# A first item of the expert phase with a table of its own, and five more split tiles: one core of Trainium2

## The chip, the cores and the metric

The kernel runs on one core of a Trainium2 chip. The core has five engines that run their own instruction streams in order and wait for each other by semaphores: TensorE (PE in the profile; its weight loads are PEld), VectorE (DVE), ScalarE (ACT), GpSimd (POOL) and SyncE (SP), of which SP and POOL issue the transfers here. The metric is the time of one execution on the device, in microseconds (us).

## What is computed

Four batches of attention across channels (B = 4, N = 3648 rows, C = 256 channels), and on its 14592 output rows a mixture of 16 experts, each row going to one of them:

```python
qn = q / (norm(q, axis=1) + 1e-06); kn = k / (norm(k, axis=1) + 1e-06)
s = kn.transpose(0, 2, 1) @ qn / tau            # 256 x 256 for each batch
a = softmax(s); x = (v @ a).reshape(B * N, C)
g = argmax(x @ w_group); e = argmax(x @ w_expert[g])    # one of 4 x 4 experts for each row
out[row] = p_group * p_expert * (relu(x[row] @ w1[g, e]) @ w2[g, e])
```

## The kernel before

**Units.** A batch is cut into 28 tiles of 128 rows and one of 64, four tiles to a unit; a batch has eight units (GPB = 8), of which the last holds the 64 rows. Units are counted through, 0 to 31; batch 2 is units 16 to 23, batch 3 units 24 to 31.

**Phase 1, on unit u.** s_load (L184) loads q and k of the unit into `qkraw`. s_split (L198, L199) takes some of its tiles apart into a high and a low half: ACT writes the high half and DVE subtracts. Tile 3 (SPLIT) goes to `qkhi`/`qklo`; the tiles listed in MORE go to `hh`/`hl`, of which there are three buffers. ACT squares the unit, and s_add (L216) adds the squares up in `sqa`. s_mm (L232) multiplies into `sacc`: a raw tile by two fp32 matmuls, which are four records in the trace, a split one by three matmuls of halves for each of two column blocks. At the end of a batch softmax has several steps: `ssq` on DVE (L243, L244) sums the squares, `nps` on PE (L247, L249) adds them over the partitions, `rn` takes the root and the reciprocal, `sm` scales `sacc`, and behind that come the exponentials and the weights `ahi`, `alo`.

**Phase 2, on unit x, ten units later.** x_load (L306) loads v, x_tr (L318 to L320) transposes it on PE into `vtr` and splits it into `vth` and `vtl`, and x_mm (L342) multiplies with `ahi` and `alo`; ACT copies the result to `xs` (L345). The routing (L369 to L439, DVE mostly) finds each row's expert and its place in the buffer x_sorted; it runs over ranges of tiles, in batch 2 over (0, 8), (8, 20) and (20, 29). `carry` counts the rows of each expert. The scatters (L466, POOL) write one tile of rows each into x_sorted.

**Phase 3.** The first items of 512 rows of one expert are chosen before all rows are routed. When the ranges up to (2, 20) are through (PRE), tables_pre makes the table tb_pre of four items (KPRE = 4): each full 512 rows of an expert give one. fetch_w (L677, L684) loads an item's weights and fetch_x (L697, L698) its rows of x_sorted; SP reads expert and place from the table first. The reads of these items wait for the scatters of the ranges below PRE, one for each tile: 29 of each of batches 0 and 1 and 20 of batch 2, which is 78. Later scatters are declared harmless to them. split_x (L779 to L781) transposes item 0's rows into `xtr` and splits them, split_w (L741, L742) splits its weights, and ffn1 (L930, `hmm`) and ffn2 (L950 to L959) follow.

**What sets the order.** The streams of SP and POOL are written out by hand throughout. PE, ACT and DVE are ordered by the scheduler up to step 30 (TM), which covers units 0 to 29 of phase 1, the sums and `ssq` of the last batch, and units 0 to 19 of phase 2; `sqa` and `ssq` of the last unit stand there under a raised priority (tc.high_priority, offset 400). Then all five engines run in the order of the code, and PE's first instructions there are `nps` of the last batch, the transposes of v and the matmuls of units 30 and 31.

Of the kernel before, what the change touches and what calls it, by code (L numbers as in the profile page):

```python
# [46 lines left out]

PRE = (2, 20)
assert 2 * NT + PRE[1] * P > E * (BIG - 1) + (KPRE - 1) * BIG
# [3 lines left out]
PLAIN = (GPB + 1, GPB + 2)  # L53
MORE = {**{u: (2,) for u in range(GPB + 6, 28)}, 28: (1, 2), 29: (0, 1, 2), 30: (0, 1, 2)}
US = UX = B * GPB
# [6 lines left out]
def attention_moe(ctx: ExitStack, tc, q, k, v, tau, w_group, w_expert, w1, w2, out):  # L62
# [288 lines left out]

    scatters, pend, now, rows_at, early, spread = [], [], [0], {}, [], []

# [94 lines left out]

    before = lambda r: r < PRE
    late = []  # L450

    def scatter(n, wait=0):
        for _ in range(n):
            if not pend or pend[0][1] + wait > now[0]:
                break
            (b, j0), _, j, si = pend.pop(0)
            g, t = divmod(j0 + j, GJ)
            rows, nj = rows_of(g)
            xs = rows_at[b, g]
            if t == 0:  # L460
                tok = xs[:, 0:nj, C].bitcast(I32)
                if g < NG:
                    POOL.iota(tok, pattern=[[-1, GJ]], base=NOID - b * NT - g * GJ, channel_multiplier=-J)
                else:
                    POOL.iota(tok, pattern=[[0, 1]], base=NOID - b * NT - J * P, channel_multiplier=-1)
            ins = POOL.indirect_dma_start(  # L466
                out=xs_d, out_offset=bass.IndirectOffsetOnAxis(ap=si[:rows, j:j + 1], axis=0),
                in_=xs[:rows, t, 0:RW].bitcast(I32), in_offset=None, bounds_check=NSLOT - 1, oob_is_err=False)
            if not before((b, j0)):
                for o in early:  # L470
                    tc.declare_no_dep(ins.ins, o, reason="the first items' slots have been filled")
                late.append(ins.ins)
            for o in scatters:
                tc.declare_no_dep(ins.ins, o, reason="every token has a slot of its own")
            scatters.append(ins.ins)
            pause()
# [80 lines left out]
    used = r16("used")  # L557

    def tables_pre():
        cnt = carry  # L560
        f = shifted(cnt, 9, "f1", "key")
        inc = r16("inc1", "order")
        DVE.tensor_tensor_scan(inc, onesf[:, 0:E], f, 0.0, ALU.mult, ALU.add)
        DVE.tensor_tensor(inc, inc, f, ALU.subtract)
        yield
        DVE.tensor_scalar(inc, inc, -1.0, float(KPRE), ALU.mult, ALU.add)
        DVE.tensor_scalar(inc, inc, 0.0, None, ALU.max)
        DVE.tensor_tensor(used, inc, f, ALU.min)
        full = r16("held1", "full")
        DVE.tensor_scalar(full, used, float(BIG), None, ALU.mult)  # L570
        yield
        return (yield from table_steps(KPRE, used, ecap, full, BIG, "pre"))

    def zero_rows():
# [3 lines left out]
        DVE.tensor_tensor(end, end, own, ALU.mult)  # L578
        ends = rp.tile([P, 1], F32, name="ends")
        DVE.tensor_reduce(ends, end, AX.X, ALU.add)  # L580
# [4 lines left out]
                                in_=zero[:3 * E, :].bitcast(I32), in_offset=None, bounds_check=NSLOT - 1, oob_is_err=False)  # L585
        for o in scatters + early:
            tc.declare_no_dep(ins.ins, o, reason="these slots have no token")
        scatters.append(ins.ins)
        late.append(ins.ins)

# [95 lines left out]
    def fetch_x(d, tb, i):  # L686
# [5 lines left out]
        d["nv"] = tb[1][:, i:i + 1]  # L692
        if tb is not tb_pre:
            gather(d["xg"].rearrange("p t w -> p (t w)"), tb[2][:, i:i + 1], 4)
            pause()
            return
        s = SP.value_load(tb[0][0:1, i, 1:2], min_val=0, max_val=DUMMY)  # L697
        ins = SP.dma_start(d["xg"].bitcast(I32), xs_d[ds(s, BIG), :].rearrange("(p t) w -> p t w", t=4))  # L698
        early.append(ins.ins)
        for o in late:  # L700
            tc.declare_no_dep(ins.ins, o, reason="the first items' slots have been filled")

# [100 lines left out]
    xs_at = {t: t - XOFF if t >= XOFF else None for t in range(UX + XOFF)}  # L803
    tb_pre = tb_big = tb_pc = tb_sub = nsub = None

# [5 lines left out]
    def queue(x):  # L811
        b, g = divmod(x, GPB)
        for j0, j1 in RANGES[b]:
            if (b, j1) != (B - 1, NJ) and j1 == min(NJ, (g + 1) * GJ) and (g < NG - 1 or j1 == NJ):
                if not (j1 == NJ and g == NG - 1):
                    rgens.append(routing(b, j0, j1))
                    if (b, j1) == PRE:
                        rgens.append(pre_gen())
# [49 lines left out]
    def where(i):  # L868
        return (items[i], tb_pre, i) if i < KPRE else (items[i], tb_big, i - KPRE)

# [14 lines left out]
    for t in range(TM, len(xs_at)):  # L885
# [18 lines left out]
        if k == 8:  # L904
            fetch_w(items[0], tb_pre, 0, "w1")
            fetch_x(items[0], tb_pre, 0)
            fetch_w(items[0], tb_pre, 0, "w2")
        if k == 10:
            vx_.close()
            wb = ctx.enter_context(tc.tile_pool(name="wb", bufs=4))  # L910
        if x == UX - 1:
            fetch_x(items[1], tb_pre, 1)
            fetch_w(items[1], tb_pre, 1, "w1")
            split_x(items[0])
# [465 lines left out]
```

## Time and profile before

| | |
|---|---|
| time, median of three runs | 929.68 us (926.58, 929.68, 929.70) |
| the profiled execution | 926.72 us, span 924.9 us |
| granted clock of TensorE, mean | 0.996 |
| PE, PEld, DVE, ACT, POOL busy | 99%, 84%, 77%, 53%, 44% of the span |

The profile is of one execution. A row of waits gives the time that an engine stood idle before a line and what released it; a row of the timeline gives start, duration, engine, line, output and input, and in brackets the idle time ahead of it. The ends of matmuls are modelled, so their starts are the better measure. PEclk is the granted clock of TensorE as a share of full speed.

### The profile page before, as it was taken

How to read it: one execution, taken by the hardware profiler on the slowest of the kernel's cores; microseconds unless marked ns; L12 is line 12 of the kernel's file. 1: busy time of each engine (PE TensorE's matmuls, PEld its weight loads, DVE VectorE, ACT ScalarE, POOL GpSimd, SP SyncE). 2: the span in 40 equal slices, each digit the busy share in tenths (PEclk: the TensorE clock that was granted, in tenths of full speed). 3: DMA queues.
4: the chain of work that ended last, by engine and by line, in shares of the span. 5: the costliest groups of instructions: out<-in, count | busy, mean ns of one | idle time of the engine just before them, and what ended most of it. 6: DMA issues, size and time to landing. Idle time of an engine off the chain costs nothing.

```text
span 924.9 us, 17250 instructions
## 1 busy us (share of the span) xinstructions
PE 911.8 (99%) x5660; PEld 773.7 (84%) x5660; DVE 715.0 (77%) x1496; ACT 494.7 (53%) x831; POOL 403.8 (44%) x569
## 2 busy tenths in 40 slices
PE   8999999999999999999999999999999999999997
PEld 7899999999899988888888888888888888888885
DVE  6888999888799877967885777678776877587752
ACT  6788888777454444444444444444544444444432
POOL 0001898888588663323222333343334333332222
PEclk9999999999999999999999999999999999999998
DMA  9975779274855676767777777777777677667750
GB/s 310 353 285 193 264 263 319 95 248 144 294 195 175 193 250 225 232 228 235 248 249 239 257 251 246 249 245 232 227 223 244 224 250 233 220 236 241 244 165 32
DMA packets 159172, 213.97 MB, mean 231 GB/s; under 512 B 63107, under 2 KB 117643, under 8 KB 159072
## 3 DMA queue, kind: packets, MB, share of 16 engines
q1 hardware_dynamic: 144128, 168.23, 56.0%
q0 software_dynamic: 14944, 44.54, 12.8%
q8 instruction: 46, 0.75, 0.3%
q14 instruction: 54, 0.44, 0.2%
HBM read 170.33 MB, written 31.39 MB: 218 GB/s over the span
## 4 chain that ended last, share of the span: by engine, by line
PE 90%; DVE 3%; ACT 3%; DMA 2%; issue 1%; SPq 0%; POOL 0%; DVEq 0%; ACTq 0%
PE hmm L930 34%; PE wacc L950 19%; PE wacc L951 10%; PE xmm L342 7%; PE sacc L232 6%; PE yacc L959 5%; PE qacc L1067 2%; PE qmm L1054 2%; PE vtr L318 2%; DMA qkraw<-in_k 2%; DVE sqa L216 1%; ACT xs L345 1%; ACT sq L207 1%; PE xtr L779 1%; DVE vtl L320 1%
## 5 line engine op out<-in xcount | busy, mean ns | idle before, releaser
L939 ACT ACTIVATE hh<-hmm 128x512 fp32r<-128x512 f32 x222 | 133.4, 601 | 351.7 <-PE hmm L930 347.3
L930 PE MATMUL hmm<-xth,ww 128*128 128x512 f32 x896 | 317.6, 395 | 0.0
L979 POOL DMA_INDIRECT out<-ys,ids x112 | 132.9, 1187 | 386.7 <-DVE ys L968 357.6
L950 PE MATMUL wacc<-ww,hh 128*128 128x512 f32 x752 | 274.6, 399 | 0.0
L940 DVE SCALAR_TENSOR_TENSOR hl<-hmm,hh 128x512 fp32r<-128x512 f32 x222 | 152.7, 690 | 128.4 <-ACT hh L939 125.7
L951 PE MATMUL wacc<-ww,hl 128*128 128x256 f32 x752 | 210.8, 280 | 0.0
L930 PEld LDWEIGHTS hmm<-xth,ww 128*128 128x128 f32 x896 | 168.8, 188 | 38.1
L930 PE MATMUL hmm<-xtl,ww 128*128 128x512 f32 x448 | 177.7, 397 | 0.0
L950 PEld LDWEIGHTS wacc<-ww,hh 128*128 128x128 f32 x752 | 141.3, 188 | 43.0 <-DVE ys L968 8.2
L466 POOL DMA_INDIRECT x_sorted<-xs,si x112 | 137.2, 1225 | 56.9 <-DVE si L439 25.5
L742 DVE TENSOR_TENSOR ww<-wraw,ww 128x1024 fp32r<-128x1024 f32 x112 | 136.7, 1221 | 16.6 <-ACT ww L741 15.4
L951 PEld LDWEIGHTS wacc<-ww,hl 128*128 128x128 f32 x752 | 142.1, 189 | 7.2
L741 ACT ACTIVATE ww<-wraw 128x1024 fp32r<-128x1024 f32 x112 | 118.8, 1060 | 6.2 <-DMA wraw<-in_moe_w 6.1
L930 PEld LDWEIGHTS hmm<-xtl,ww 128*128 128x128 f32 x448 | 84.5, 189 | 9.7
L159 POOL MEMSET zero<- 128x256 f32 x260 | 87.1, 335 | 0.1
L232 PE MATMUL sacc<-qkraw 128*128 128x256 f32 (+1 forms) x280 | 69.5, 387 | 1.1 <-DMA qkraw<-in_k 1.1
L342 PE MATMUL xmm<-ahi,vth 128*128 128x276 f32 (+1 forms) x232 | 69.5, 304 | 0.3 <-ACT xs L345 0.3
L342 PE MATMUL xmm<-alo,vth 128*128 128x276 f32 (+1 forms) x232 | 67.8, 293 | 0.0
L342 PE MATMUL xmm<-ahi,vtl 128*128 128x276 f32 (+1 forms) x232 | 67.5, 292 | 0.0
L216 DVE TENSOR_TENSOR sqa<-sqa,sq 128x1024 f32<-128x1024 f32 (+3 forms) x46 | 59.9, 1309 | 6.1 <-ACT sq L207 3.8
L1039 DVE STREAM_TRANSPOSE qhT<-qh 32x128 f32<-32x128 f32 x192 | 57.7, 300 | 2.7
L232 PEld LDWEIGHTS sacc<-qkraw 128*128 128x128 f32 (+1 forms) x280 | 50.5, 192 | 7.8 <-issue 2.2
(276 smaller groups left out, 1357.2 us busy)
## 6 DMA issues: line engine op xcount, KB each, us to landing
wraw<-in_moe_w SPq DMA_DIRECT2D x55, 1024.0 KB
wraw<-in_moe_w SPq DMA_DIRECT2D x50, 512.0 KB
qw<-in_moe_w SPq DMA_DIRECT2D x48, 512.0 KB
vr<-in_v SPq DMA_DIRECT2D x28, 512.0 KB
qkraw<-in_q SPq DMA_DIRECT2D x26, 512.0 KB
qkraw<-in_k SPq DMA_DIRECT2D x26, 512.0 KB
xq<-xg SPq DMA_DIRECT2D x368, 32.0 KB
x_sorted<-xs,si POOLq DMA_INDIRECT x112, 3.9
```

The source lines that it names most:

```text
L159: POOL.memset(zero[:, 0:256], 0.0)
L232: PE.matmul(d["acc"][:, c, :], kt[:rows, 1, cs], qt[:rows, 0, :], start=d.pop("first", True) and c == 0, stop=(g == NG), skip_group_check= ...
L342: PE.matmul(mm[:rows, :NE], vt[:, c, j * P:j * P + rows], at[:, c, :], start=(n == 0), stop=(n == 5))
L466: ins = POOL.indirect_dma_start(out=xs_d, out_offset=bass.IndirectOffsetOnAxis(ap=si[:rows, j:j + 1], axis=0), in_=xs[:rows, t, 0:RW].bitc ...
L741: ACT.activation(h, r, AF.Copy)
L742: DVE.tensor_tensor(l, r, h, ALU.subtract)
L930: PE.matmul(mm, wt[:, c, fs], xt[:, c, :], start=(n == 0), stop=(n == 5))
L939: ACT.activation(hh, mm, AF.Relu)
L940: d["hl"] = DVE.scalar_tensor_tensor(hl, mm, 0.0, hh, ALU.max, ALU.subtract)
L950: PE.matmul(d["acc"][t].rearrange("p c n -> p (c n)"), hh[:, tsl], d["w2w"][:, f, :], start=(f == 0), stop=(f == 7), skip_group_check=True)
L951: PE.matmul(d["acc"][t][:, 0, :], hl[:, tsl], d["w2h"][:, f, :], start=False, stop=(f == 7), skip_group_check=True)
L979: ins = POOL.indirect_dma_start(out=out, out_offset=bass.IndirectOffsetOnAxis(ap=d["ids"][:, t:t + 1], axis=0), in_=d["ys"][:, t, :], in_o ...
```

## The change

Two edits. First, the table of item 0 is made earlier. After the routing of (2, 8), when the rows of 58 + 8 = 66 tiles are counted, table_first finds the first expert that has 512 rows (`ge0`, a running count, `one` marks that expert) and writes tb_first. Item 0 is read by that table, and its read waits for the scatters of the ranges below PRE0 = (2, 8) alone. tables_pre makes three items, from what is left when the rows of item 0 are taken off. Second, MORE has tile 1 as well in units 24 to 27 and tile 0 as well in unit 28, so that five tiles more run over halves.

```diff
-PRE = (2, 20)
+PRE0, PRE = (2, 8), (2, 20)
+assert 2 * NT + PRE0[1] * P > E * (BIG - 1)
-MORE = {**{u: (2,) for u in range(GPB + 6, 28)}, 28: (1, 2), 29: (0, 1, 2), 30: (0, 1, 2)}
+MORE = {**{u: (2,) for u in range(GPB + 6, 24)}, **{u: (1, 2) for u in range(24, 28)}, 28: (0, 1, 2), 29: (0, 1, 2), 30: (0, 1, 2)}
...
-            if not before((b, j0)):
-                for o in early:
+            for o, limit in early:
+                if (b, j0) >= limit:
                     tc.declare_no_dep(ins.ins, o, reason="the first items' slots have been filled")
-                late.append(ins.ins)
+            late.append((ins.ins, (b, j0)))
...
+    def table_first():
+
+        ge = r16("ge0", "order")
+        DVE.tensor_scalar(ge, carry, float(BIG), None, ALU.is_ge)
+        inc = r16("inc0", "key")
+        DVE.tensor_tensor_scan(inc, onesf[:, 0:E], ge, 0.0, ALU.mult, ALU.add)
+        DVE.scalar_tensor_tensor(one, inc, 1.0, ge, ALU.is_equal, ALU.mult)
+        DVE.tensor_tensor(ge, one, iof[:, 0:E], ALU.mult)
+        e0 = rp.tile([P, 1], F32, tag="ends", name="e0")
+        DVE.tensor_reduce(e0, ge, AX.X, ALU.add)
+        tb = rp.tile([P, 1, 2], I32, name="tb_first")
+        DVE.tensor_copy(tb[:, :, 0], e0)
+        DVE.tensor_scalar(tb[:, :, 1], e0, float(CAP), None, ALU.mult)
+        yield
+        return tb, full0
...
     def tables_pre():
-        cnt = carry
-        f = shifted(cnt, 9, "f1", "key")
+        f = r16("f1", "held2")
+        DVE.tensor_tensor(f, shifted(carry, 9, "key"), one, ALU.subtract)
...
-        return (yield from table_steps(KPRE, used, ecap, full, BIG, "pre"))
+        first = r16("first", "s0")
+        DVE.scalar_tensor_tensor(first, one, float(BIG), ecap, ALU.mult, ALU.add)
+        yield
+        tb = yield from table_steps(KPRE - 1, used, first, full, BIG, "pre")
+        DVE.tensor_tensor(used, used, one, ALU.add)
+        return tb
...
-        early.append(ins.ins)
-        for o in late:
-            tc.declare_no_dep(ins.ins, o, reason="the first items' slots have been filled")
+        limit = PRE0 if d is items[0] else PRE
+        early.append((ins.ins, limit))
+        for o, r in late:
+            if r >= limit:
+                tc.declare_no_dep(ins.ins, o, reason="the first items' slots have been filled")
...
                     rgens.append(routing(b, j0, j1))
+                    if (b, j1) == PRE0:
+                        rgens.append(first_gen())
...
     def where(i):
-        return (items[i], tb_pre, i) if i < KPRE else (items[i], tb_big, i - KPRE)
+        if i == 0:
+            return items[i], tb_first, 0
+        return (items[i], tb_pre, i - 1) if i < KPRE else (items[i], tb_big, i - KPRE)
```

The order of the instructions moves with it. The lines of the changed kernel are one higher than before up to the scatters.

On DVE, before, near the end of the part that the scheduler orders: the sums of squares of the last batch (L243, L244, `ssq`) stand among the routing of (2, 8), and the routing, the splits of v (`vtl`) and of q and k follow.

```order
L243 TENSOR_TENSOR sqa<-sqa 128x2x512
L378 SCALAR_TENSOR_TENSOR oh_2381<-z,key_99 128x160
L400 TENSOR_REDUCE sw<-ez 128x40
L379 TENSOR_REDUCE m_2377<-oh_2381 128x40
L244 TENSOR_TENSOR ssq<-sqa 128x512
L380 TENSOR_TENSOR oh_2381<-oh_2381,m_2377 128x160
L320 TENSOR_TENSOR vtl<-vtr,vth 128x512
```

The last rows of that part on DVE, before: splits of q and k and the end of the routing (`si`), and then the first row in hand order (`rn`).

```order
L199 TENSOR_TENSOR hl<-qkraw,hh 128x512
L434 TENSOR_TENSOR inc<-inc,oh 128x128
L199 TENSOR_TENSOR hl<-qkraw,hh 128x512
L437 TENSOR_REDUCE sf<-inc 128x8
L199 TENSOR_TENSOR hl<-qkraw,hh 128x512
L439 CAST si<-sf 128x8
L255 TENSOR_SCALAR rn<-rn 128x258
```

The same place on DVE now: the last sums and `ssq` (L217, L244, L245) stand behind the splits, the routing and the new table.

```order
L200 TENSOR_TENSOR hl<-qkraw,hh 128x512
L571 TENSOR_REDUCE e_2582<-ge_2576 128x1
L200 TENSOR_TENSOR hl<-qkraw,hh 128x512
L573 CAST tb_first<-e_2582 128x1
L574 TENSOR_SCALAR tb_first<-e_2582 128x1
L217 TENSOR_TENSOR sqa<-sqa,sq 128x1024
L217 TENSOR_TENSOR sqa<-sqa,sq 64x256
L244 TENSOR_TENSOR sqa<-sqa 128x2x512
L245 TENSOR_TENSOR ssq<-sqa 128x512
L256 TENSOR_SCALAR rn<-rn 128x258
```

What moved: `ssq` went from 24 rows ahead of the end of that part to its last row.

On PE, now, with its waits: the last matmuls of unit 19, then `nps`, which reads `ssq`, the transposes of v and the matmuls of unit 30.

```order
L343 MATMUL xmm<-ahi,vtl 128x276
L248 MATMUL nps<-ssq,onesf 128x256 [waits DVE_49]
L250 MATMUL nps<-onesf,ssq 128x1 x2
L319 MATMUL vtr<-ident,vr 128x128 [waits DMAHW0_49,PE_49]
L319 MATMUL vtr<-ident,vr 128x128 x3
L319 MATMUL vtr<-ident,vr 128x128 [waits PE_49]
L319 MATMUL vtr<-ident,vr 128x128 x3
L233 MATMUL sacc<-hh 128x256
```

What moved: nothing in the rows; the DVE row that `nps` waits for is the one that moved above.

On SP, before: the second half of item 0's weights and, behind it, the read of item 1's rows from x_sorted.

```order
L682 DMA wraw<-in_moe_w 128x4x256
L682 ISA
L682 DMA wraw<-in_moe_w 128x4x256 [waits DMAHW6_49]
L697 TENSOR_LOAD tb_pre
L697 ISA x2
L698 ISA
L698 DMA xg<-x_sorted 128x1088 [waits DMAHW7_49,DVE_49,Pool_49]
```

The same place on SP now.

```order
L705 DMA wraw<-in_moe_w 128x4x256
L705 ISA
L705 DMA wraw<-in_moe_w 128x4x256 [waits DMAHW6_49]
L720 TENSOR_LOAD tb_pre [waits DVE_49]
L720 ISA x2
L721 ISA
L721 DMA xg<-x_sorted 128x1088 [waits DMASW4_49,DMASW3_49,DMASW5_49,DMASW2_49,DMASW6_49,DMASW1_49,DMASW7_49,DMASW0_49,DMAHW7_49,DVE_49,Pool_49]
```

What moved: the waits for POOL's transfers (DMASW) of the range (8, 20) and for tb_pre stand at item 1 now; item 0's read keeps waits of that kind, for earlier transfers.

## Rows read from the trace of the kernel before

**Rows 1.** The page, busy time of each engine: us, share of the span, instructions.

```profile
PE 911.8 (99%) x5660; PEld 773.7 (84%) x5660; DVE 715.0 (77%) x1496; ACT 494.7 (53%) x831; POOL 403.8 (44%) x569
```

**Rows 2.** Waits of PE, 140 to 340 us: total, times, longest.

```profile
PE xtr L779 <- DMA wraw<-x_sorted: 3.1, 1, 3.1
PE vtr L318 <- DVE vtl L320: 0.3, 1, 0.3
PE atp L281 <- DVE ax L275: 0.2, 1, 0.2
```

**Rows 3.** Chain of work that ended last, 200 to 240 us: start, duration, what.

```profile
226.37 2.44 DMA x_sorted<-xs,si
...
229.08 4.03 DMA wraw<-x_sorted
...
233.25 1.39 PE xtr L779 x8
```

**Rows 4.** Windows: length; PE, PEld, DVE, ACT, POOL busy; PEclk; DMA share; GB/s.

```profile
233.20:234.00 0.80, 0.75 (x6) 0.78 (x7) 0.00 (x0) 0.00 (x0) 0.80 (x1) 1.00 0.96 302
234.00:235.00 1.00, 1.00 (x7) 0.99 (x7) 0.37 (x1) 0.92 (x2) 0.83 (x3) 0.54 0.96 290
235.00:236.00 1.00, 1.00 (x6) 0.98 (x5) 1.00 (x4) 0.28 (x1) 0.93 (x3) 0.50 1.02 230
236.00:237.00 1.00, 1.00 (x4) 0.81 (x3) 0.93 (x5) 0.61 (x2) 0.79 (x1) 0.50 0.92 333
237.00:238.00 1.00, 1.00 (x5) 0.72 (x5) 0.49 (x1) 0.00 (x0) 0.83 (x3) 0.75 1.05 406
```

**Rows 5.** Timeline of POOL: the scatter of the 66th tile.

```profile
207.91 0.97 POOL L466 DMA_INDIRECT x_sorted<-xs,si  x1 [0.16 <-DVE f L554]
```

**Rows 6.** Timeline of SP's queue: the last loads of v; item 1's read.

```profile
188.21 19.82 SPq L306 DMA_DIRECT2D vr<-in_v  x8
...
232.18 0.35 SPq L698 DMA_DIRECT2D xg<-x_sorted  x1
```

**Rows 7.** Timeline of DVE, 226 to 239 us: item 0's weights and tokens are split.

```profile
229.27 2.46 DVE L742 TENSOR_TENSOR ww<-wraw,ww 128x1024 fp32r<-128x1024 f32 x2 [0.58 <-ACT ww L741]
234.63 1.37 DVE L781 TENSOR_TENSOR xtl<-xtr,xth 128x512 fp32r<-128x512 f32 x2 [2.90 <-ACT xth L780]
```

**Rows 8.** Timeline of PE: two raw tiles of q and k, then matmuls of halves.

```profile
147.79 1.89 PE L232 MATMUL sacc<-qkraw 128*128 128x256 f32 x8
...
149.63 0.28 PE L232 MATMUL sacc<-hl,hh 128*128 128x256 f32 x1
149.75 0.28 PE L232 MATMUL sacc<-hh,hl 128*128 128x256 f32 x1
```

**Rows 9.** Windows ahead of nps, columns as in rows 4.

```profile
160.00:170.00 10.00, 10.00 (x80) 9.85 (x80) 9.93 (x30) 6.85 (x16) 9.06 (x12) 1.00 0.46 174
170.00:180.00 10.00, 9.91 (x82) 9.54 (x81) 9.82 (x30) 7.25 (x17) 9.07 (x12) 1.00 0.24 86
180.00:182.00 2.00, 2.00 (x17) 2.00 (x17) 1.90 (x6) 0.98 (x3) 1.83 (x3) 1.00 0.20 72
```

**Rows 10.** Timeline of DVE, 140 to 205 us.

```profile
173.96 0.67 DVE L244 TENSOR_TENSOR ssq<-sqa 128x512 f32<-128x512 f32 x1
...
178.91 0.15 DVE L431 TENSOR_TENSOR carry<-pp,carry 128x16 f32<-128x16 f32 x1
178.99 0.15 DVE L432 SCALAR_TENSOR_TENSOR bs<-bs,ecap 128x16 f32<-128x16 f32 x1
...
181.14 0.67 DVE L199 TENSOR_TENSOR hl<-qkraw,hh 128x512 fp32r<-128x512 f32 x1
181.73 0.17 DVE L439 CAST si<-sf 128x8 int32<-128x8 f32 x1
```

**Rows 11.** Timeline of PE: nps of the last batch.

```profile
182.39 0.59 PE L247 MATMUL nps<-ssq,onesf 128*128 128x256 f32 x2
```

**Rows 12.** Timeline of ACT: a high half that waited for its buffer.

```profile
164.06 1.29 ACT L198 ACTIVATE hh<-qkraw 128x512 fp32r<-128x512 f32 x2 [1.17 <-PE sacc L232]
```

More of the change, by code (lines that the diff above doesn't have):

```diff
@@ L349, in x_mm @@
         ACT.activation(Lx, xs[:rows, :nj, C:NE], AF.Copy)
-    scatters, pend, now, rows_at, early, spread = [], [], [0], {}, [], []
+    scatters, pend, now, rows_at, early, late, spread = [], [], [0], {}, [], [], []
     def bc(x, n):
@@ L447, in routing @@
         yield
-    before = lambda r: r < PRE
-    late = []
     def scatter(n, wait=0):
@@ L557, in attention_moe @@
     used = r16("used")
+    one = r16("one", "up")
+    full0 = cp.tile([P, 1], F32, name="full0")
+    DVE.memset(full0, float(BIG))
+    def table_first():
[12 more added lines that the diff above has]
+        return tb, full0
     def tables_pre():
-        cnt = carry
-        f = shifted(cnt, 9, "f1", "key")
+        f = r16("f1", "held2")
+        DVE.tensor_tensor(f, shifted(carry, 9, "key"), one, ALU.subtract)
         inc = r16("inc1", "order")
@@ L565, in tables_pre @@
         yield
-        DVE.tensor_scalar(inc, inc, -1.0, float(KPRE), ALU.mult, ALU.add)
+        DVE.tensor_scalar(inc, inc, -1.0, float(KPRE - 1), ALU.mult, ALU.add)
         DVE.tensor_scalar(inc, inc, 0.0, None, ALU.max)
@@ L578, in zero_rows @@
         DVE.tensor_tensor(end, end, own, ALU.mult)
-        ends = rp.tile([P, 1], F32, name="ends")
+        ends = rp.tile([P, 1], F32, tag="ends", name="ends")
         DVE.tensor_reduce(ends, end, AX.X, ALU.add)
@@ L585, in zero_rows @@
                                 in_=zero[:3 * E, :].bitcast(I32), in_offset=None, bounds_check=NSLOT - 1, oob_is_err=False)
-        for o in scatters + early:
+        for o in scatters + [o for o, _ in early]:
             tc.declare_no_dep(ins.ins, o, reason="these slots have no token")
         scatters.append(ins.ins)
-        late.append(ins.ins)
+        late.append((ins.ins, (B, 0)))
     def tables_rest():
@@ L692, in fetch_x @@
         d["nv"] = tb[1][:, i:i + 1]
-        if tb is not tb_pre:
+        if all(d is not o for o in items[0:KPRE]):
             gather(d["xg"].rearrange("p t w -> p (t w)"), tb[2][:, i:i + 1], 4)
@@ L803, in attention_moe, with first_gen @@
     xs_at = {t: t - XOFF if t >= XOFF else None for t in range(UX + XOFF)}
-    tb_pre = tb_big = tb_pc = tb_sub = nsub = None
+    tb_first = tb_pre = tb_big = tb_pc = tb_sub = nsub = None
+    def first_gen():
+        nonlocal tb_first
+        tb_first = yield from table_first()
     def pre_gen():
@@ L904, in attention_moe @@
         if k == 8:
-            fetch_w(items[0], tb_pre, 0, "w1")
-            fetch_x(items[0], tb_pre, 0)
-            fetch_w(items[0], tb_pre, 0, "w2")
+            fetch_w(*where(0), "w1")
+            fetch_x(*where(0))
+            fetch_w(*where(0), "w2")
         if k == 10:
@@ L911, in attention_moe @@
         if x == UX - 1:
-            fetch_x(items[1], tb_pre, 1)
-            fetch_w(items[1], tb_pre, 1, "w1")
+            fetch_x(*where(1))
+            fetch_w(*where(1), "w1")
             split_x(items[0])
```

## The prediction

> **What bounds the kernel now.** I read the busy table of the page first: TensorE (PE) is busy 99% of the span [rows 1]. So an edit pays only where it takes idle time or work off PE, and it costs only where it gives PE some. Next I read the waits of PE from 140 to 340 us, where the two phases meet. Two of the three waits are 0.3 us or less; the third, 3.1 us, is on item 0's tokens, the transposes `xtr` behind the read of x_sorted [rows 2]. The chain of waits tells why they are late: the 78th scatter starts at 226.37 and takes 2.44 us, the read goes out behind it and takes 4.03, and `xtr` starts at 233.25 [rows 3]. The window table gives the second half of the price. PE's granted clock was 1.00 in the stretches up to 234 us and is 0.54, 0.50, 0.50 and 0.75 in the four microseconds behind the wait [rows 4]: half of 2.4 GHz is 1.2 GHz, and 0.46 + 0.50 + 0.50 + 0.25 = **1.7 us** of full-speed work is lost there. The place thus costs 3.1 + 1.7 = 4.8 us, and it is what the first edit is about.
>
> **Part 1: the earlier table and the earlier read remove about 4.2 us.** Item 0's read now waits for 66 scatters, not for 78. The 66th starts at 207.91 [rows 5], and with the 2.44 us of the other one [rows 3] it has landed at 210.4. SP is free for item 0 behind the last loads of v, at 188.21 + 19.82 = 208.0 [rows 6]; its expert number is in tb_first, which DVE writes directly behind the routing of (2,8), whose last row is at 181.73 [rows 10], long before SP comes to it. With 4.03 us for the read it is in SBUF near 215, and PE asks for it at 230.1: some 15 us of cover, and a shift of all of that by 5 us is the same for PE and scatter. What is late next? DVE splits item 0's w1 until 229.27 + 2.46 = 231.73, and only then can it take the tokens' low half, 1.37 us for two or 0.69 for the first [rows 7]; the FFN's second matmul needs that at 232.4. PE has 1.39 us of transposes [rows 3] and six matmuls of the last 64 rows ahead of it, some 0.4 us more at full clock, and stands there at 230.1 + 1.8 = 231.9. So about 0.6 us of wait remains. Sum: -(3.1 + 1.7) + 0.6 = **-4.2 us**. PE waits nowhere else up to 340 us [rows 2], so all of it would reach the end of that stretch, and PE's 99% leaves little room behind it.
>
> What stands behind the moved wait: on SP, the wait for the 78th scatter goes from item 0's read to item 1's, and w2 of item 0 goes out some 18 us earlier. Item 1's read was issued at 232.18 and can now go behind the 78th scatter, at 229.1 in the clock of before [rows 3, 6], plus whatever PE and DVE have shifted. Its tokens are split six FFN steps later. I cost that at nothing; its cover is those six steps of item 0, and without them one read, 4.0 us, would show. The loads of v that take over phase 1's space wait for DVE's last work on it and so come as much later as DVE does; PE, which wants them, is late by about as much (Part 3), so they are at nothing too.
>
> **Part 2: five more split tiles, PE.** A raw tile is four fp32 records on PE. Two raw tiles and one fp32r matmul go from 147.79 to 149.63, and one fp32r matmul follows another by 0.12 us [rows 8]: (1.84 - 0.12) / 2 = 0.86 a raw tile. A split one is six of 0.12, 0.72. Five tiles: 5 x 0.14 to 0.15 = **-0.7 us** of PE ahead of nps. ACT gets five copies more and has the room (7.25 of 10 us busy at 170 to 180, [rows 9]).
>
> **Part 3: what both edits put on DVE, and who waits for it.** DVE is full there: 9.82 of 10 us at 170 to 180 and 1.90 of 2 up to 182 [rows 9]. Each split tile adds a subtraction, `hl`, of 0.59 us from start to start (181.14 to 181.73, [rows 10]): 5 x 0.59 = 3.0. table_first adds seven small operations; two such follow each other by 0.08 us (178.91 to 178.99), so 7 x 0.08 = 0.6. Together **3.6 us** on an engine without gaps.
>
> This would be hidden if nobody waited for DVE's last operations. In the order of before, `ssq` of the last batch stands 24 rows ahead of the end of what the scheduler orders; it ends at 173.96 + 0.67 = 174.6, and nps on PE, at 182.39, finds it done for 8 us [rows 10, 11]. In the changed order the scheduler has put the last squares' sums and `ssq` **behind** all routing, splits and the table: `ssq` is DVE's last operation there. The set of operations ahead of the cut is the same apart from the 3.6 us, so it ends where `si` ended, 181.73 + 0.17 = 181.9 [rows 10], plus 3.6: 185.5. PE, in order and 0.7 us early, stands before nps at 182.39 - 0.74 = 181.65 and idles 3.8 us. Behind it on PE are the transposes of v, the last two units of q and k, and every later matmul, so against before all is late by 185.5 - 182.4 = **+3.1 us** (Part 2's gain is inside it). That idle time is longer than the 3.1 us behind which the clock went to half in before, so I add the same **+1.7 us**.
>
> Of this price the trace has one instance: the fall from 1.00 to 0.50 behind 3.1 us of idleness, and full speed again at 238 us with PE busy throughout [rows 2, 4]; by it the sum is +0.6. The Trainium skill (TensorE: Matmul & The Clock Gate, Part 1: The HAM clock gate) speaks against a fixed price: a monitor of the engine's recent activity halves the clock and gives it back, and the number of matmuls at the lower clock differs between runs of one kernel. No run here shows that yet; by it the sum lies anywhere from -1.1, no matmul slowed, to +0.6.
>
> **The sum.** -4.2 + 3.1 + 1.7 = **+0.6 us**: the idle gap moves from 230 us to 182 us and keeps its size. The profiled execution took 926.72 us (span 924.9); the same with the change would take 927.3. The median of the runs is 929.68, with one run at 926.58 beside two at 929.7, so the profile is of the faster sort; on the median the sum gives 930.3. I take the middle of the two, rounded, **928.9 us**.
>
> **Bounds of the unknown costs.** The trace of before shows no wait at nps, so its size is bounded from both sides. Low: DVE fills the gaps that it has from 160 to 182, 0.07 + 0.18 + 0.10 = 0.35 us [rows 9]; the shift is then 2.7 us, the idle time 3.4, and the fall of the clock need not follow: -4.2 + 2.7 = -1.5, 925.1 from the fastest run. High: DVE itself may have to wait for the copies it subtracts. `hh` has three buffers, and ACT has waited 1.17 us for PE to free one [rows 12]; unit 28 needs three at once where it needed two. Two such waits put the end of `ssq` at 185.5 + 2.3 = 187.8, the shift at 5.4: -4.2 + 5.4 + 1.7 = +2.9, 932.6 from the median. I take the middle since ACT has a quarter of its time free.
>
> **Rivals.** About 0.5%, 4.65 us, is what a measurement of this kernel can tell from no change.
> 1. *No wait at nps.* If DVE fills its gaps or `ssq` comes through in time, only the gains stay: -4.2 - 0.7 = -4.9 us, 921.8 on the profile and 924.8 on the median. For it: DVE's pace also depends on what feeds it, and PE, ACT and DVE are paced by each other. Against: DVE has 0.35 us of gaps in the 22 us ahead [rows 9], and its order is fixed. The sum is just over the bound of 4.65, so three quarters of this case count as faster.
> 2. *A wait without the fall of the clock.* -4.2 + 3.1 = -1.1: 925.6 to 928.6. The idle time is at 3.8 longer than the 3.1 that did it once, but one instance is no law.
> 3. *The splits wait for each other (slower).* With `hh` and `hl` in three buffers, DVE's last `hl`s wait for ACT, ACT for PE's matmuls on an older tile, and PE stands at nps: units 30 and 31 come behind nps on PE, so their halves can't be freed until `ssq` is done. If the scheduler's order puts many of them ahead of `ssq`, each round adds a copy and a subtraction, 0.65 + 0.60 = 1.25 us. Net loss over 4.65 us begins where the shift passes 4.65 + 4.2 - 1.7 = 7.2 us, that is with four more rounds than I counted: 3.1 + 5 = 8.1, sum +5.6, 932.3 on the profile and 935.3 on the median. For it: unit 30 and 28 both hold three tiles. Against: before has the same ring with the same three for units 29 and 30 and DVE shows no gap of that size.
> 4. *The change does not do what it says.* If item 0's read stays late (by a wait that the scatters of other tokens still bring, or by SP standing at another load), the 4.8 us stay and the shift at nps comes on top, since the scatters come later with DVE and PE: up to 3.1 + 1.7 = +4.8, at the edge of slower, 931.5 to 934.5. Against: SP's order shows the wait for these scatters gone from item 0's row and present at item 1's.
>
> **How the numbers follow.** The forecast, +0.6 with its bounds -1.5 to +2.9: 0.58. Rival 1: 0.16, of which 0.12 ends faster than the bound. Rival 2: 0.12. Rival 3: 0.08, all slower. Rival 4: 0.06, half of it slower. So faster 0.12, slower 0.11, within 0.5%: 0.77. The range for 8 in 10 takes the forecast with its bounds, rival 2, and the inner part of rivals 1 and 4: from 924.8 (rival 1 on the median, just below 925.1) to 932.6 (the median plus 2.9).
>
> **What the changed profile would show.** Right: PE's waits from 140 to 340 us have no row of 3 us at `xtr` and one of 3.5 to 4 us at nps behind DVE's `ssq`; the dip of the granted clock stands at 186 to 190 us and not at 234 to 238; DVE is busy without gaps up to 185.5; the read of item 0 goes out near 211 to 216. Part 1 is wrong if `xtr` still waits more than 1 us or if item 1's tokens bring a new wait. Part 3 is wrong if nps waits under 2 us or over 6. A time under 924 means that the wait at nps did not come; one over 934 that DVE waited for its copies.

## The result

| | median of ten runs, us | lowest to highest |
|---|---|---|
| before | 929.0 | 926.5 to 930.5 |
| after | 934.1 | 932.4 to 935.8 |

The ratio after to before is 1.0062, interval 1.0048 to 1.0075: the changed kernel is slower by about 5 us. That is outside the range of the prediction (924.8 to 932.6), on the side of rival 4, and beyond the half per cent that a measurement tells apart. The profiled execution of after took 935.79 us, span 934.1. One execution of all that the experiments timed stands apart, 1699.58 us at a mean clock of 0.857 in the run with the table early and the read late; the ratios leave it out.

### The profile page after: what moved, and what is told of

It is laid out like the page before. It is cut to its first block, busy times and chain, and to the rows that moved or that the text cites. A ratio compares the mean times of both kernels' runs of the same rounds, so it can differ in the third digit from the quotient of the medians.

```text
span 934.1 us, 17294 instructions
## 1 busy us (share of the span) xinstructions
PE 916.2 (98%) x5670; PEld 774.6 (83%) x5670; DVE 718.3 (77%) x1512; ACT 495.7 (53%) x836; POOL 401.5 (43%) x569
## 4 chain that ended last, share of the span: by engine, by line
PE 85%; issue 6%; DVE 3%; POOL 2%; ACT 2%; DMA 0%; POOLq 0%; SPq 0%; DVEq 0%; ACTq 0%
PE hmm L963 30%; PE wacc L983 17%; PE sacc L233 9%; PE wacc L984 8%; PE xmm L343 7%; PE yacc L992 5%; PE vtr L319 2%; PE qmm L1087 2%; PE qacc L1100 2%; POOL out L1012 2%; ACT xs L346 1%; DVE vtl L321 1%; DMA qkraw<-in_k 0%; POOL zero L160 0%; PE xtr L804 0%
## 5 line engine op out<-in xcount | busy, mean ns | idle before, releaser
L465 POOL DMA_INDIRECT x_sorted<-xs,si x112 | 135.2, 1207 | 65.5 <-issue 33.9
L233 PE MATMUL sacc<-qkraw 128*128 128x256 f32 (+1 forms) x260 | 64.7, 389 | 0.5 <-DMA qkraw<-in_k 0.5
L217 DVE TENSOR_TENSOR sqa<-sqa,sq 128x1024 f32<-128x1024 f32 (+3 forms) x46 | 59.9, 1308 | 5.0 <-ACT sq L208 2.7
L346 ACT ACTIVATE xs<-xmm 128x276 f32<-128x276 f32 x112 | 42.6, 410 | 30.4 <-PE xmm L343 17.7
```

The source lines that it names most:

```text
L233: PE.matmul(d["acc"][:, c, :], kt[:rows, 1, cs], qt[:rows, 0, :], start=d.pop("first", True) and c == 0, stop=(g == NG), skip_group_check= ...
L465: ins = POOL.indirect_dma_start(out=xs_d, out_offset=bass.IndirectOffsetOnAxis(ap=si[:rows, j:j + 1], axis=0), in_=xs[:rows, t, 0:RW].bitc ...
```

## The profile after

The busy line of the page, as [rows 1]; then the waits of PE, 140 to 340 us, columns as in [rows 2].

```profile
PE 916.2 (98%) x5670; PEld 774.6 (83%) x5670; DVE 718.3 (77%) x1512; ACT 495.7 (53%) x836; POOL 401.5 (43%) x569
```

```profile
PE nps L248 <- DVE ssq L245: 4.2, 1, 4.2
PE vtr L319 <- issue: 2.5, 2, 2.0
PE vtr L319 <- DVE vtl L321: 2.0, 3, 1.0
PE hmm L963 <- DVE xtl L806: 0.2, 1, 0.2
```

The 3.1 us at `xtr` [rows 2] are gone, and 4.2 us stand at nps, behind `ssq`, as forecast. (nps is the sum over the partitions that opens the softmax of the last batch; `vtr` are the transposes of v.) The two rows at `vtr` were in no step of the prediction. The chain of waits of after, 180 to 190 us (start, duration, what), shows what `ssq` came behind:

```profile
181.76 0.07 DVE tb_first L573
181.83 0.06 DVE tb_first L574
181.89 1.14 DVE sqa L217
...
183.50 1.24 DVE sqa L244
184.76 0.70 DVE ssq L245
...
185.51 1.22 PE nps L248 x2
```

The last squares' sums start only when the early table is written, and `ssq` ends at 185.46; the forecast said 185.5. The windows of after, columns as in [rows 4], give the clock:

```profile
180.00:185.00 5.00, 1.27 (x11) 1.05 (x9) 4.90 (x12) 2.67 (x5) 4.66 (x3) 0.90 0.17 57
185.00:190.00 5.00, 4.49 (x19) 4.31 (x20) 2.59 (x3) 2.56 (x5) 4.39 (x8) 0.50 0.25 87
190.00:200.00 10.00, 10.00 (x75) 9.47 (x74) 5.45 (x13) 4.63 (x14) 8.61 (x17) 0.96 0.62 218
```

PE does 1.27 us of work in the first five, and all that it does up to 190 runs at half clock. The timeline of SP's queue of after (start, duration, what) shows the early read and item 1's:

```profile
218.92 0.00 SPq L721 DMA_DIRECT2D wraw<-x_sorted  x1
...
233.28 0.35 SPq L721 DMA_DIRECT2D xg<-x_sorted  x1
```

Item 0's read goes out at 218.92, 2.9 us behind the forecast's 211 to 216 and long before PE asks. So every part does in the main what the prediction said, and yet the sum is off by some 4.5 us. Either the wait at nps costs more than 4.8, or the early read brings less than 4.2, or something costed at nothing has a price; item 0's w2, which is now loaded while v is read, and the five splits were the suspects. These are the theories that the experiments set against each other.

## The experiments

The experiments ran in five groups, each on one chip, and all ratios are against the kernel before in the same group. That matters, for in the median before took 929.0 us in the result and 923.3, 924.3, 928.3, 923.9 and 925.1 in the five groups, the last three on one chip. The changed kernel was timed again in the third group, 934.68 (1.0073, interval 1.0052 to 1.0094), and in the fourth, 929.99 (1.0058, 1.0039 to 1.0078). The loss is 5.1 to 6.4 us in these three medians; the one execution of the first group was 7.9 us above before's median.

**One part alone.** The table without the splits has MORE of before; the splits without the table have PRE, the table and the reads of before:

```diff
-MORE = {**{u: (2,) for u in range(GPB + 6, 24)}, **{u: (1, 2) for u in range(24, 28)}, 28: (0, 1, 2), ...}
+MORE = {**{u: (2,) for u in range(GPB + 6, 28)}, 28: (1, 2), 29: (0, 1, 2), 30: (0, 1, 2)}
```

**`ssq` early.** The splits, squares and sums of unit 30 get the raised priority that those of unit 31 have, so that `ssq` stands some 26 rows ahead of the end of what the scheduler orders. The order of the splits moves with it, so this kernel has waits of its own, which are shown below:

```diff
-        s_split(t + 1)
+        with tc.high_priority(offset=400) if t + 1 >= 30 else ExitStack():
+            s_split(t + 1)
...
-        s_add(t + 1)
+        with tc.high_priority(offset=400) if t + 1 >= 30 else ExitStack():
+            s_add(t + 1)
```

First group, one execution of after and three kernels in rounds:

> The changed kernel as it is, a second look. Its first profile shows the wait at nps behind ssq (4.2 us) and then a second loss that the prediction did not have: PE is 5.7 us late at 197 us and 12.1 us late at 236 us against before, with waits of PE at the transposes of v of 0.5 to 2.0 us that end on no visible event. Theory A (the second loss belongs to the kernel): the same waits again, PE again 5 to 7 us later at 236 us than at 197 us. Theory B (a chance of that execution, or of its recording): nps waits 4 us again, and behind 197 us PE loses less than 2 us more. Time 932.4 to 935.8 by either.

Measured: 931.18, under the range of both theories. nps waits 4.2 us again, the transposes of v only 1.0 us in all, and between the end of phase 1 and `xtr` PE loses 1.1 us more than in before: theory B.

> The early table and the early read of item 0, with the split tiles of before (MORE as before); ssq stands ahead of the last routing and splits as before. Theory A1 (the wait at nps is the loss, and the second loss follows from it): no wait at nps, no wait at xtr, 4.2 us faster than before, 924 to 925.5. Theory A2 (the second loss comes from what the early table itself sets free: the weights and rows of item 0 are loaded from 217 us on while the last units of v are multiplied): the wait at xtr is gone, but waits of some 5 us at the transposes of v take its place, 929 to 931.

Measured: 925.11, 1.0020 (1.0009 to 1.0031). The wait at `xtr` is gone and 2.0 us stand at `vtr`: neither A1 (4.2 us faster) nor the full A2.

> The five more split tiles alone, with the table and the read of item 0 as before; ssq is DVE's last operation ahead of nps here too. Theory A1: nps waits some 3.5 us for ssq and the clock falls there, the wait at xtr stays at 2 to 3 us: 3 to 6 us slower than before, 932 to 935, with the second loss. Theory A2: the wait at nps and its clock, but no waits at the transposes of v: 932 to 934.

Measured: 928.06, 1.0057 (1.0038 to 1.0076). nps waits 3.7 us; the wait at `xtr`, which A1 kept, is gone too.

> The changed kernel, with the splits and the sums of squares of unit 30 under the same raised priority as those of unit 31: ssq stands 26 rows ahead of the end again and all splits and the early table stay. Theory A1: no wait at nps, 4.9 us faster than before: 923.5 to 925. Theory A2: no wait at nps, but the waits at the transposes of v of 4 to 6 us stay: 928 to 931. If DVE's last splits of unit 30 come too late for PE instead, a wait of 1 to 3 us at sacc behind nps, 925 to 928.

Measured: 928.00, 1.0050 (1.0033 to 1.0067), the time of A2, with 3.4 us of waits at `vtr`.

The table alone gained nothing, and with the wait at nps gone after was still slow. In these traces ACT also stood idle for 1 to 2 us several times between 200 and 232 us while PE had long begun what it waited for, and I took the earlier w2 for the cause. The second group moved that load back behind item 1's read, and in one kernel let item 0's read wait for all 78 scatters again:

```diff
         if k == 8:
             fetch_w(*where(0), "w1")
             fetch_x(*where(0))
-            fetch_w(*where(0), "w2")
...
             fetch_x(*where(1))
+            fetch_w(*where(0), "w2")
```

```diff
-        limit = PRE0 if d is items[0] else PRE
+        limit = PRE
```

> The kernel before as it is, for a profile taken on the same chip as those of the experiments. In the first runs of the experiments it took 923.3 us, 6 us less than where the prediction was made. Theory B1 (the chip differs at the place that the change removes): the wait at xtr is under 2 us here, or the clock does not fall there, so that the early read has less to remove. Theory B2 (the chip differs elsewhere): the wait at xtr is 3 us with the clock at half for some 3 us, as before, and the time is saved elsewhere.

Measured: 926.77. `xtr` waits 2.7 us and the clock is at half for 6.8: nearest to B2.

> The early table and the early read of item 0 without the five splits, and item 0's w2 loaded behind item 1's read, that is behind the 78th scatter as before and not some 15 us earlier. Theory C1 (the 1 MB of w2, moved ahead of PE's last units of v, slows ACT's copies and the transposes there): the waits of PE at the transposes of v fall from 2.0 us to under 0.5 and the kernel gains 1.5 to 3 us on the early table alone (925.1): 922 to 923.5. Theory C2 (w2 has no part in it): 924.5 to 925.5, the same waits.

Measured: 923.94, 1.0000 (0.9987 to 1.0013), between C1 and C2; PE now waits 0.9 us for item 0's `ww`.

> The changed kernel with ssq early (as in the run with the sums of unit 30 raised, 928.0) and item 0's w2 behind item 1's read. Theory C1: 2 to 4 us faster than with ssq early alone: 924 to 926. Theory C2: 927.5 to 928.5.

Measured: 925.67, 1.0021 (1.0008 to 1.0034), in the range of C1.

> The early table without the five splits, but item 0's read waits for the 78th scatter as before (so w2 stands behind it too): only DVE's seven operations, the other order of the experts and the later tables are left of the first edit. Theory C1: no waits at the transposes of v, the wait at xtr as in the kernel before: 923 to 924.3. Theory C3 (the table itself, or the experts' new order in the long phase, costs what the early read gains): 925 to 927, slower than the early read.

Measured: 924.62, 1.0001 (0.9985 to 1.0016), between C1 and C3. `xtr` waits 1.4 us, with the clock at 1.00 behind it.

No kernel of this group showed ACT's pauses, not even the ones whose edit had nothing to do with them. So the third group asked whether they belong to a kernel at all:

> The changed kernel as it is, beside the next three on one chip. Its first two profiles show, besides the wait at nps, that ACT stands still for 1 to 1.8 us several times between 200 and 232 us though PE's matmuls ahead of it have started long before; so do the profiles of the early table alone, of the splits alone and of ssq early, but not those of the second set of runs, which came from another chip. Theory D1 (the early load of w2 brings these gaps): they are there again, PE is 12 us later than before at the last unit of v or at least 3 us later than at nps. Theory D2 (the gaps go with a chip or a recording, not with the kernel): a profile here has them only if that of the kernel before has them too, and PE's loss stays what nps and its clock make it: 3.1 us and 2.5 to 3.4 us. Time by both 5 to 8 us above the kernel before.

Measured: 934.68, 1.0073 (1.0052 to 1.0094), with pauses.

> The early table and the early read without the five splits, again, to stand beside the run with w2 late on one chip. D1: 1.5 to 3 us slower than with w2 late, with ACT's gaps at the transposes of v. D2: within 0.7 us of the run with w2 late, without such gaps where the kernel before has none.

Measured: 929.86, 1.0017 (1.0006 to 1.0027), with pauses.

> The early table and read without the five splits, and item 0's w2 behind item 1's read, again. D1 and D2: as the kernel before to within 1 us (0.4 us less in its first run); D1: 1.5 to 3 us faster than the run with w2 early.

Measured: 928.87, 1.0015 (1.0001 to 1.0029), with pauses; 1.0 us below the early w2 in the median and level with it by the ratios, where D1 had 1.5 to 3 us.

> The kernel before, for its profile on this chip. D1: no gaps of ACT over 0.7 us between 200 and 230 us, here or anywhere. D2: gaps here if the other three have them. As for the clock: the profiles so far had it at half for 3.4 and for 6.8 us behind the wait at xtr, at mean clocks of 0.996 and 0.994; more than half of the timed runs had a mean clock of 0.998 to 0.999 and took 921.5 to 924.9 us. If the mean is 0.998 or more here, no half clock at xtr and 922 to 924 us.

Measured: 925.99 at a mean clock of 0.999. The theory of the early w2 falls here: the kernel before has the pauses too, and made late by them it has no wait at `xtr`. The timeline of ACT in this run (start, duration, what; in brackets the idle time and what ended it):

```profile
211.14 0.40 ACT L345 ACTIVATE xs<-xmm 128x276 f32<-128x276 f32 x1 [1.08 <-PE vtr L318]
212.64 0.40 ACT L345 ACTIVATE xs<-xmm 128x276 f32<-128x276 f32 x1 [1.09 <-PE xmm L342]
```

And the same kernel in the second group, at the same place, with idle times of 0.3 us:

```profile
212.86 0.40 ACT L345 ACTIVATE xs<-xmm 128x276 f32<-128x276 f32 x1 [0.30 <-PE xmm L342]
213.61 0.40 ACT L345 ACTIVATE xs<-xmm 128x276 f32<-128x276 f32 x1 [0.35 <-PE xmm L342]
```

The pauses are in the profile of after above (not in that of before beside it), in all four of the first group, where before was not profiled, and in all four of the third, before among them; they are in none of the other groups, not even with after (the fourth). So they go with no kernel. What makes them stays open. It follows that the row `vtr` behind issue in the profile of after above, and half of that behind `vtl`, are no work of the change: the profile of after in the fourth group does not have them.

The fourth group crossed the two parts with the place of `ssq`, all on one chip:

> The changed kernel beside the next three on one chip. F1 (the wait at nps and the half clock behind it are most of the loss): 5 to 8 us above the kernel before, mean clock 0.994 to 0.997 in every run. F2 (most of it is the splits' work on DVE, wherever it stands): as much.

Measured: 929.99, 1.0058 (1.0039 to 1.0078), 6.1 us above before.

> The changed kernel with ssq early. F1: no wait at nps, mean clock 0.998, 3 us or more faster than the changed kernel, within 2 us of the early table alone, that is 1.5 to 3.5 us above the kernel before. F2: 4 to 6 us above the kernel before, less than 2 us faster than the changed kernel.

Measured: 926.13, 1.0018 (1.0005 to 1.0031), as F1.

> The five splits alone, without the new table, with ssq early (the same raised priority). F1: within 1.5 us of the kernel before. F2: 3 to 5 us above it.

Measured: 924.89, 1.0004 (0.9993 to 1.0016), as F1.

> The five splits alone, with ssq last as the scheduler puts it. Its first run was 5.3 us above the kernel before on a chip where that took 923.3. F1: 3.5 to 6 us above the kernel before, and 3 us or more above the same with ssq early. F2: less than 2 us above the same with ssq early.

Measured: 927.40, 1.0039 (1.0027 to 1.0052), 2.5 us above the same with `ssq` early: between F1 and F2.

| median, us (before 923.86) | `ssq` behind | `ssq` early | price of the wait at nps |
|---|---|---|---|
| splits alone | 927.40 | 924.89 | 2.5 |
| splits and table | 929.99 | 926.13 | 3.9 |
| what the table adds | 2.6 | 1.2 | |

So taking the wait at nps away gives back 3.9 of the 6.1 us that after lost in this group, and the splits with `ssq` early are level with before within the interval. By the ratios it is 3.7 of 5.4, the splits' price is 3.2, and the table adds 1.8 and 1.3. The third row is the surprise: the early table and read, forecast at -4.2, **add** 1.2 to 2.6 beside the splits.

These prices are net, for `ssq` early has waits that before lacks: PE idles 0.4, 0.5 and 1.3 us ahead of 178 us, in both profiles. In that of the splits alone the clock fell behind them, in that of after it did not. Windows of the two, in this order:

```profile
179.00:182.00 3.00, 3.00 (x16) 3.00 (x16) 2.65 (x6) 1.39 (x4) 2.72 (x4) 0.50 0.25 88
```

```profile
179.00:182.00 3.00, 2.90 (x23) 2.56 (x23) 2.87 (x10) 1.25 (x3) 2.72 (x4) 1.00 0.26 96
```

So the 2.5 us of the splits are rather too small. The last group took the table alone once more, beside a profile of before:

> The early table and the early read without the five splits, once more: its two runs were 1.6 and 1.9 us above the kernel before, in calls whose profiles show gaps of ACT, and w2 late was level with before. G1 (what the early read takes away, the wait of 2.7 to 3.1 us, is real, and the new table gives most of it back in the long phase and at the transposes of v): within 1.5 us of the kernel before, in the profile no wait at xtr and PE 2 to 3 us earlier at the first FFN matmul than where the clock fell. G2 (the gaps that those calls showed belong to this kernel): 1.5 us or more above it, with gaps.

Measured: 923.99 against 925.08, 0.9992 (0.9981 to 1.0003), as G1.

> The kernel before, one more profile. In the timed runs of the last call 16 of 29 had a mean clock of 0.998 or more and took 921.6 to 925.0 us, the others 0.996 or 0.997 and up to 927.9. If the mean is 0.998 or more here: no half clock behind xtr, 922 to 924 us, whether or not PE waits there. If it is 0.997 or less: half clock behind xtr for 3.4 or 6.8 us and 925 to 927 us.

Measured: 927.12, mean clock 0.997, 2.9 us at `xtr` and half clock for 3.4 us, near what was expected.

## Why the prediction was wrong, step by step

**Part 3, the wait at nps: right in place and size.** PE's waits and windows in the profile of after without pauses (fourth group):

```profile
PE nps L248 <- DVE ssq L245: 4.2, 1, 4.2
PE vtr L319 <- DVE vtl L321: 1.0, 1, 1.0
PE hmm L963 <- DVE xtl L806: 0.2, 1, 0.2
```

```profile
181.00:185.40 4.40, 0.24 (x2) 0.02 (x1) 4.30 (x9) 1.95 (x3) 4.24 (x3) 0.81 0.10 32
185.40:190.60 5.20, 5.12 (x22) 4.95 (x23) 2.75 (x5) 2.85 (x5) 4.52 (x9) 0.50 0.24 84
190.60:200.00 9.40, 9.40 (x73) 8.87 (x72) 5.07 (x13) 4.34 (x13) 8.08 (x15) 1.00 0.68 234
```

And with `ssq` early (the waits at `vtr`, the first of them at 177.7 us, then the same two windows):

```profile
PE vtr L319 <- issue: 1.3, 1, 1.3
PE vtr L319 <- DVE vtl L321: 0.7, 1, 0.7
```

```profile
181.00:185.40 4.40, 4.40 (x40) 4.38 (x39) 3.97 (x9) 3.54 (x8) 4.07 (x6) 1.00 0.20 67
185.40:190.60 5.20, 5.20 (x39) 4.67 (x38) 3.75 (x6) 3.95 (x7) 4.43 (x9) 1.00 0.24 84
```

Idle time 4.2 against 3.8 forecast, shift of nps against before 185.5 - 182.4 = 3.1 as forecast. **The clock behind it was sized too small.** I carried over the 1.7 us of the instance at `xtr`. Here the clock is at 0.50 until 190.6 us, with PE at work in 5.1 us of it: 2.5 us lost, against 1.7. The other three profiles of after have PE at work for 5.4, 6.5 and 6.2 us at half clock, so the term is 2.5 to 3.3. Rival 2 (no fall of the clock) is out in all four profiles, and all 23 executions of after had a mean clock of 0.994 to 0.997. The bound above (DVE waits for its copies, rival 3 further out) did not come: DVE has no gap worth naming before `ssq`. The sign "over 934: DVE waited for its copies" misled, for the median of the result was 934.1 without such a wait.

**Part 1, the early read: this term failed, -4.2 us booked and next to nothing found.** The read does go out early and the wait at `xtr` is gone; that all of it would reach the end of the kernel is the step that was wrong. The kernel before in the last group, waits and windows of PE:

```profile
PE xtr L779 <- DMA wraw<-x_sorted: 2.9, 1, 2.9
```

```profile
232.00:234.00 2.00, 0.40 (x3) 0.43 (x4) 0.36 (x1) 0.00 (x0) 1.67 (x4) 1.00 0.60 180
234.00:236.00 2.00, 2.00 (x12) 1.98 (x12) 0.88 (x2) 1.20 (x2) 1.83 (x3) 0.56 0.96 318
236.00:238.00 2.00, 2.00 (x8) 1.66 (x7) 1.90 (x7) 0.61 (x2) 1.72 (x4) 0.59 1.02 332
```

The table alone, same group, with the reads of items 0 and 1 from SP's timeline:

```profile
PE vtr L319 <- DVE vtl L321: 0.7, 1, 0.7
PE hmm L963 <- ACT xth L805: 0.3, 1, 0.3
```

```profile
232.00:234.00 2.00, 1.50 (x8) 0.81 (x6) 1.67 (x5) 1.58 (x4) 1.84 (x3) 1.00 0.01 4
234.00:236.00 2.00, 2.00 (x10) 1.65 (x9) 1.90 (x7) 1.12 (x2) 1.83 (x3) 1.00 0.88 328
```

```profile
211.28 0.35 SPq L721 DMA_DIRECT2D wraw<-x_sorted  x1
...
226.30 0.35 SPq L721 DMA_DIRECT2D xg<-x_sorted  x1
```

The read goes out at 211.28 where I said 211 to 216, the wait and the half clock are gone. In time, little came of it: the table with the read early (and w2 late, which costs 0.9 us at `ww`) took 923.94 us and with the read late 924.62 in the same group, 0.7 apart. What then became of the 4.2 us? Starts and ends from the timelines of PE, us (with `ssq` early nps stands elsewhere in PE's order, so its start is left out):

| | nps starts | phase 1 ends | first `hmm` | last `hmm` | between them | span |
|---|---|---|---|---|---|---|
| before, first profile | 182.4 | 188.2 | 235.8 | 912.0 | 676.2 | 924.9 |
| before, last group | 183.0 | 188.8 | 236.3 | 912.4 | 676.0 | 925.3 |
| table alone, last group | 182.5 | 188.3 | 232.7 | 909.6 | 676.9 | 922.2 |
| splits alone | 184.8 | 192.3 | 236.4 | 912.7 | 676.4 | 925.2 |
| splits, `ssq` early | | 191.0 | 235.0 | 911.0 | 676.0 | 924.1 |
| after, fourth group | 185.5 | 193.8 | 238.2 | 916.2 | 678.0 | 928.9 |
| after, `ssq` early | | 189.8 | 234.1 | 912.1 | 678.0 | 924.9 |

1. *In the profiles the gain is there, and part of it is given back.* The first `hmm` of the table alone starts 3.6 us earlier than in before; at the last one 2.8 are left, at the end of the span 3.1. The three kernels with the new table take 676.9 to 678.0 us between the two, those without it 676.0 to 676.4. Part of that is fixed: from the 101st to the 1101st `hmm` all seven profiles of kernels without the new table take 508.22 us, and the thirteen with it 508.77 (ten of them) to 509.09. The run with the read late is among the ten (676.4 us from the first to the last), so this 0.55 us goes with the new table and not with the early read or the splits; whether by the items that it picks or by something else that moved with it, no run took apart. In the two at 678.0, 0.8 and 0.6 us are lost at one place near 830 us, where three other profiles with the new table lose 0.3 to 0.7 and none without it does.
2. *`vtl` is not free.* With either part PE waits 0.6 to 1.0 us for DVE's `vtl` where before has 0.3 [rows 2]; I had put v's loads at nothing.
3. *The profiled execution was probably not typical.* I took 3.1 + 1.7 us at `xtr` from one execution. In the groups that ran before 17 times (the last) and 29 times (the fourth), its mean clock was 0.998 or 0.999 in 8 and in 19 of them (not 16, as the last expectation has it), at medians of 923.6 and 923.2 us; with a lower clock the medians were 925.9 and 925.9. In the first two groups it was 15 of 17 and 15 of 29. In the third it was 15 of 23, and there the two sorts took the same, 928.3 and 928.2. Three profiles of before show the wait and a half clock around or behind it for 3.4 to 6.8 us, at mean clocks of 0.994 to 0.997; the one at 0.999 has neither. The mean clock is a sign and no proof, for it also holds a fall at the end of the span that every profile has, 3.4 to 6.9 us long. If it tells rightly, before does not pay the full price in about half of its executions or more, and the median hardly holds what the early read removes. The table alone, at 0.998 or more in all its timed executions of three groups, lies at 923.99 in the last, beside before's 923.6 with a full clock and 925.9 without. Whether before still waits at `xtr` when its clock stays up isn't shown; the one such profile was of a group with ACT's pauses.
4. *Beside the splits there is nothing left for the early read to gain.* I wrote that a shift is "the same for PE and scatter". It isn't, when it comes from nps: PE is late by what `ssq` adds, the scatters are not by as much. The splits alone, waits of PE and item 0's read on SP's timeline, which goes out at 229.08 and 229.66 in the two profiles of before in the table:

```profile
PE nps L247 <- DVE ssq L244: 3.7, 1, 3.7
PE vtr L318 <- DVE vtl L320: 0.6, 1, 0.6
PE hmm L930 <- DVE xtl L781: 0.2, 1, 0.2
```

```profile
230.19 0.35 SPq L698 DMA_DIRECT2D wraw<-x_sorted  x1
```

The read is at most 1.1 us later than in before, and there is no row at `xtr`: a PE that is some 4 us late at the end of phase 1 finds the tokens in SBUF. Its first `hmm` and its end (236.4 and 925.2) stand level with before's, so what the prediction booked as a gain of the table comes without any table. What is left of the table then is its cost: the wait at nps is 4.2 instead of 3.7 us, the clock there costs 2.5 instead of 1.7 (3.4 us at half clock in the splits alone), together 1.3, and the long phase is about 1 us longer. That is 2.3 us where the fourth group's medians show 2.6 and its ratios 1.8, and the second part alone is near the 1.2 that they show with `ssq` early.

The Trainium skill (TensorE: Matmul & The Clock Gate, Part 1: The HAM clock gate) says that the number of matmuls at the lower clock differs between runs of one kernel. The trace agrees: the three profiles of before with the wait at `xtr` have half clock there for 3.4, 6.8 and 3.4 us. I had let it widen the sum; the right use was to ask how often the one instance comes.

**The sum by what was measured,** in the profile of after without pauses against the profile of [rows 1 to 12]: 3.1 at nps, 2.5 of clock and 0.7 at `vtl` make PE 6.3 late at unit 31; what before loses at `xtr` and after doesn't is 3.9, so the first `hmm` is 2.4 late; the long phase adds 1.8 (0.55 of it the fixed part and 0.8 at the one place near 830 us); what follows the last `hmm` gives back 0.2. That is 928.9 against 924.9, +4.0 where I had +0.6: 0.8 by the clock, 0.7 by `vtl`, 0.3 by the smaller gain, 1.6 behind it. The measured +5.1 to +6.4 is 1 to 2.4 more. Point 3 would give it, and in the second and last groups the median of before does stand 2.4 and 2.0 us below its profiled execution; but in the result and in the third group it stands 2.3 above, so this remainder is argued and not shown. (In the prediction's own sum the middle of 927.3 and 930.3 is 928.8, not 928.9; nothing hangs on it.)

**Rivals.** Rival 1 fell with the wait at nps, rival 2 with the clock behind it. Rival 3 didn't occur. Rival 4 had the right size, "up to +4.8", and the wrong mechanism: the read is early as written. Part 2's gain fits: PE came to nps at 185.51 - 4.23 = 181.3, 1.1 us ahead of the first profile of before, where I had said 0.7. But before itself starts nps anywhere from 181.5 to 183.0 in its four profiles, so a gain of this size isn't told from chance.

No version beat the kernel before: the nearest are the table alone (0.9992 to 1.0020 over three groups) and the table with w2 late (1.0000 and 1.0015).

## What to carry to other kernels

When an edit adds work to an in-order engine whose order a scheduler sets, look at which operation now stands last there and who waits for it: here a priority on one group of operations was worth 2.5 to 3.9 us, more than either part of the edit brought in any run. A stall in one profile is an instance; before its removal is booked, see whether other executions of the same kernel have it (the mean clock of each run hinted at it here, in four groups of five). And an edit that removes a stall is worth nothing beside one that makes the same engine late ahead of it, so long as what it waits for comes by another road.

## What the runs showed of the hardware

In the three profiles of before in which PE waits 2.7 to 3.1 us at `xtr`, the clock was at half for 3.4, 6.8 and 3.4 us; with 1.4 us of wait there (the read late) it stayed up. Behind 3.7 us at nps it was at half for 3.4 us in both profiles (1.7 us lost), around 4.2 us for 6.8 us in all four, of which PE was at work for 5.1 to 6.5 (2.5 to 3.3 lost). All four profiles with `ssq` early have the same two waits, 0.5 us at 176 and 1.3 us at 178 us, and in one of them the clock fell behind these, for 3.4 us. These four kernels differ in the table and in w2's place, but idleness of one size came with and without a fall, so one profile doesn't give its price.

The work between the 101st and the 1101st `hmm`, some 508 us, repeats to 0.01 us over seven profiles from different chips, so there a difference of half a microsecond is no chance. On one chip the same kernel took 928.3, 923.9 and 925.1 us in three groups, with pauses of about 1 us on ACT in the profile of the first; the cause is open.
